# Attention in a fused attention, routing and expert kernel: value products in two column tiles, scores issued three heads early, other PSUM users moved to the outputs' ring, and work moved off VectorE

## The chip, the cores and the metric

The kernel runs on one core of one Trainium2 chip. The metric is the time of one execution in device microseconds. Five engines work side by side: TensorE (PE in the profile, with its weight loads as PEld), VectorE (DVE), ScalarE (ACT), GpSimd (POOL) and SyncE (SP), which here only issues DMAs. Each engine takes its instructions in program order; what one engine needs from another is ordered by semaphores.

## The reference

```
scores = scale * q @ k^T                # 2 batches, 8 heads, 768 positions, 64 per head
keep   = (key < 4) | (0 <= query - key < 128)
a      = exp(scores - max) over keep;  a = a / (sum(a) + 1e-9)
x      = a @ v                          # laid out as 1536 tokens x 512
logits = x @ w_gate                     # 8 experts
route: walk the 12288 logits from the largest; a token takes the first expert
       that still has room (192 tokens per expert)
y      = relu(x[of e] @ w1[e]) @ w2[e]  # 8 experts, 512 -> 1024 -> 512
h      = y @ w_in;  out = (h * sigmoid(h)) @ w_out     # 512 -> 2048 -> 512
```

The inputs are float32 (`w_in` and `w_out` come as 64-bit words and are unpacked to float32 on the chip).

## The kernel before

The program has four parts one after the other: attention (`attention_band`, L196 to L484), routing by repeated counting (`Route`), the experts, and the feed-forward layer (`ffn`). While the attention runs, the first weights are loaded and unpacked.

**Tiles.** Attention works on 12 tiles of 128 queries (`NT`; i = 0 to 11, six per batch). A query block sees its own key block, the block on its left (if it is not the first of its batch, `j` = 0) and four sink keys. The loop at L441 counts heads, n = 8 i + h, one step per head, and runs on for 18 steps after the last of the 96 heads, to let the later stages finish. One step issues, for several heads at different distances behind n:

- `s_mm(n)` (L257), every fourth step: the scores of four heads, as 32 small products (16 when j = 0) in 64x64 tiles of the array, into two banks of the PSUM ring "s", which has four banks. [...]
- `s_exp(n - 2)` (L296) on ScalarE: the exponential.
- `tr(n - 5)` (L310): a transpose on TensorE into the ring "tp"; after each fourth head ScalarE copies the four results out (L321) and GpSimd masks them into a diagonal part `atd` (L323) and a left part `at` (L326).
- `s_merge` (L281) on VectorE joins the two score pieces of a head, and `s_max(n)` (L287) adds the mask and finds the maximum, one per head.
- `sink_tr` (L342): once per tile the sink weights are transposed into a bank of "s" and copied out by VectorE (`ats`, L346).
- `pv(n - 13)` (L350): the value products of one head, `d` with the own block (L361) and `f` with the left block (L363), each 128 rows by 128 columns of weights with 73 moving columns; at each fourth head one sink product for all four (L366), into a bank of the ring "X" (two banks). Then `finish` (L370): VectorE takes the reciprocal of the sums (L388), the weighted logits `lw` (L384), their sum `L` (L391) and the scaled output `x` (L395). For the last two tiles ScalarE does the scaling.
- `vw`, `vw_tr`, `sinks` (L399 to L428), at steps given by the table `VWS`: v times the gate's weights, by which the logits come with the value products. They also take their PSUM from "s" through `misc` (L330).

Small steps of VectorE and ScalarE wait in short lists (`dve_now`, `dve_bg`, `act_now`, `act_bg`, `act_late`) and are issued one or two at a time by `feed` (L430).

**The start.** VectorE clears an array `zero` (L334) that the warm-up products read (`warm`, L338): eight products of 512 columns ahead of the first scores and two at each of the next five steps (`WARM`, L193). Their results are not used.

**Loads.** All loads go through SP's queue in program order. `load` brings keys and queries of a tile, `load_v` (L213) two arrays for the values. Through `hooks` the loop also calls `Weights.load` for seven buffers, at steps 18, 20, ..., 30 (`FIRST`, L887), and `Weights.unpacked` at the 40 steps in `EVEN` and `ODD` (27 to 91), which issues one step of unpacking on VectorE: five steps (`s0` to `s4`, L930 to L949) for each of eight quarters. When a buffer is unpacked the next piece of weights is loaded into it.

**Behind the attention** the routing starts while the last tiles are still at work (`plan`, L1588), and at its end TensorE begins the experts.

Of the kernel before, what the change touches and what calls it, by code (L numbers as in the profile page):

```python
# [11 lines left out]
F32 = mybir.dt.float32  # L12
# [173 lines left out]
LT, LP, LS = 5, 13, 6  # L186
LATE = 9, 10
VWS = {8: [((0, (0,)), 0)], 10: [((0, (0,)), 1)], 11: [((0,), 2)], 13: [((0, (1,)), 0)], 16: [((0, (1,)), 1)],
       58: [((1,), 2)]}
for m in range(1, NT // 2):  # L190
    VWS[2 * H * m + 5], VWS[2 * H * m + 8] = [((m,), 0)], [((m,), 1)]
PB = {"s": 4, "tp": 2, "X": 2}
WARM = (8,) + (2,) * 5  # L193


def attention_band(tc, qd, kd, va_d, vt_d, vs_d, sel_d, wbd_d, eye_d, n_sink, ident, x_d, L_sb, pp, hooks={}):  # L196
    nc = tc.nc
    with ExitStack() as ctx:
# [14 lines left out]
        def load_v(i):  # L213
            b, j = divmod(i, NB)
            if i % 2 == 0:
                vts[i // 2] = wp.tile([P, 4, 2, P], F32, name="vt", bufs=2)
            nc.sync.dma_start(vts[i // 2][:, :, i % 2], vt_d[b, j])
            nc.sync.dma_start(va[:, j], va_d[b, j])
# [12 lines left out]
        load_v(0)  # L231
        nc.sync.dma_start(vsf[0][:96], vs_d[:96, 0])
        load_v(1)
        load(2)
        vsr = [cp.tile([97, H, VW], F32R, name=f"vsr{b}") for b in range(B)]
# [106 lines left out]
        def sink_tr(i):  # L342
            tp = misc()[:96]
            nc.tensor.transpose(tp, A.pop((i, "s")).rearrange("p r h s -> p (r h s)").bitcast(F32), ident)
            if i < NT - 1:
                dve_now.appendleft(lambda: nc.vector.tensor_copy(ats[i % 2][:96], tp))  # L346
            else:
                act_now.appendleft(lambda: nc.scalar.activation(ats[i % 2][:96], tp, AF.Copy))

        def pv(n):  # L350
            i, h = divmod(n, H)
            b, j = divmod(i, NB)
            g, r = divmod(h, 4)
            if r == 0:
                if (i, g) == (NT - 1, 0):
                    X[i, g] = misc(HH * VW).rearrange("p (h v) -> p h v", h=HH)
                else:
                    X[i, g] = pp.tile([P, HH, VW], F32, name="X", bufs=PB["X"])
# [5 lines left out]
            if r < 3:  # L364
                return
            nc.tensor.matmul(X[i, g], ats[i % 2], vsr[b][:, g * HH:(g + 1) * HH], start=False, stop=True,  # L366
# [3 lines left out]
        def finish(i, g):  # L370
# [17 lines left out]
            dve_now.append(lambda: nc.vector.reciprocal(rv, xp[:, :, D + E]))  # L388
# [1312 lines left out]
```

## Time and profile before

| | us |
|---|---|
| median of 3 runs | 551.68 (550.93 to 551.82) |
| the profiled execution, its own time | 551.16 |
| its span, first to last instruction | 549.4 |
| TensorE busy in the span | 529.3 |
| VectorE busy | 352.0 |
| ScalarE busy | 293.2 |
| GpSimd busy | 228.5 |

The profile is of one execution. Times are microseconds from the start of the span. A line such as L361 is a line of the kernel. "x24" counts instructions; a line of the timeline merges neighbours of one kind and gives the start of the first and the time until the last has ended. Instructions on one engine overlap in their ends, so what one costs in a dense stretch is the distance from its start to the next one's start, not how long it lasts. A float32 matrix product appears as two instructions. Idle time stands in brackets with what ended it.

### The profile page before, as it was taken

Reading aid. Unit: us, or ns where it says so; the run is one execution under the profiler, and the core shown is the slowest. Engines: PE = TensorE matmul, PEld = TensorE weight load, DVE = VectorE, ACT = ScalarE, POOL = GpSimd, SP = SyncE. Lnnn points to the kernel's source line nnn. Section 1 sums busy time; section 2 is a strip of 40 time slices with the busy share of each in tenths; the row PEclk is TensorE's granted clock in tenths of the full one; section 3 lists DMA queues with packets and bytes.
Section 4 is the critical chain, followed back from the end, with each engine's and each line's share of the span. In section 5 each row is a group of like instructions: output and inputs, shape, how many; then the busy total and the mean of one; then the engine's idle time right before and its main releaser. Section 6 shows DMA issues by size and latency. Waiting matters only on the chain.

```text
span 549.4 us, 10689 instructions
## 1 busy us (share of the span) xinstructions
PE 529.3 (96%) x3901; PEld 480.2 (87%) x3901; DVE 352.0 (64%) x983; ACT 293.2 (53%) x576; POOL 228.5 (42%) x219
## 2 busy tenths in 40 slices
PE   8999899878999999999999999999999999999995
PEld 4788688757999999999999998988889899888884
DVE  3798999672443443343338898777979776853523
ACT  4555555655776776786654564443544344443330
POOL 4444354377699999999992000000000000000304
PEclk9999999799999999999999999999999999999999
DMA  7999843155466666666760554553676756265502
GB/s 213 359 391 320 278 162 110 39 197 161 153 210 217 226 227 219 227 222 222 226 184 1 209 201 161 215 161 108 219 263 219 277 173 225 91 241 203 202 17 115
DMA packets 43939, 107.98 MB, mean 197 GB/s; under 512 B 4650, under 2 KB 12458, under 8 KB 43884
## 3 DMA queue, kind: packets, MB, share of 16 engines
q1 hardware_dynamic: 41696, 100.88, 54.1%
q0 software_dynamic: 1920, 6.29, 3.3%
q8 instruction: 31, 0.51, 0.4%
q14 instruction: 24, 0.20, 0.1%
q10 hardware_dynamic: 268, 0.10, 0.1%
HBM read 86.81 MB, written 20.45 MB: 195 GB/s over the span
## 4 chain that ended last, share of the span: by engine, by line
PE 69%; issue 4%; POOL 2%; DMA 1%; ACT 0%; DVE 0%; POOLq 0%; another core or an unknown queue 0%; DVEq 0%; ACTq 0%
PE h L1294 21%; PE acc L1416 21%; PE mm L1200 9%; PE m L1223 8%; PE mm L1203 4%; PE m L1226 4%; POOL out L1387 2%; PE mm L1223 1%; PE mm L1159 1%; DMA row<-x_d,idx 1%; PE mm L1226 1%; PE m L1200 0%; POOLq L1697 0%; PE m L1159 0%; ACT wr L976 0%
## 5 line engine op out<-in xcount | busy, mean ns | idle before, releaser
L979 POOL TENSOR_TENSOR wr<-raw,wr 128x1024 fp32r<-128x1024 f32 x64 | 150.8, 2386 | 9.1 <-ACT wr L976 8.9
L1416 PE MATMUL acc<-wr,gt 128*128 128x512 f32 x576 | 145.4, 395 | 0.0
L1416 PEld LDWEIGHTS acc<-wr,gt 128*128 128x128 f32 x576 | 107.3, 188 | 19.5
L1387 POOL DMA_INDIRECT out<-raw,idx x12 | 11.6, 964 | 241.4 <-DVE raw L1428 241.1
L1294 PE MATMUL h<-x,wr 128*128 128x384 f32 x528 | 101.3, 338 | 0.0
L1294 PEld LDWEIGHTS h<-x,wr 128*128 128x128 f32 x528 | 93.8, 188 | 4.0 <-DVE keep L1328 0.2
L1200 PE MATMUL mm<-xg,wr 128*128 128x384 f32 x248 | 72.4, 360 | 0.5 <-DVE xg L1174 0.3
L976 ACT ACTIVATE wr<-raw 128x1024 fp32r<-128x1024 f32 x64 | 66.8, 1052 | 2.4 <-DMA raw<-in_w 1.3
L1223 PE MATMUL m<-ht,wr 128*128 128x384 f32 x224 | 66.0, 361 | 0.0
L1203 PE MATMUL mm<-xg,wr 128*128 128x192 f32 x248 | 62.2, 251 | 0.0
L1226 PE MATMUL m<-ht,wr 128*128 128x192 f32 x224 | 56.2, 251 | 0.0
L1475 DVE TENSOR_TENSOR gt<-keep,gt 128x384 fp32r<-128x384 f32 x64 | 39.1, 612 | 26.7 <-ACT gt L1281 26.6
L301 ACT ACTIVATE A<-t,nm 128x132 f32<-128x132 f32 x96 | 36.4, 401 | 24.7 <-DVE nm L292 24.4
L1181 DVE TENSOR_TENSOR mm<-mm,t 128x384 f32<-128x384 f32 x33 | 18.7, 566 | 45.2 <-ACT t L1180 45.2
L1200 PEld LDWEIGHTS mm<-xg,wr 128*128 128x128 f32 x248 | 46.5, 188 | 1.2 <-DVE xg L1174 0.7
L1203 PEld LDWEIGHTS mm<-xg,wr 128*128 128x128 f32 x248 | 47.3, 191 | 0.0
L1280 ACT ACTIVATE keep<-keep 128x384 f32<-128x384 f32 x30 | 15.8, 526 | 54.0 <-DVE keep L1328 53.9
L1226 PEld LDWEIGHTS m<-ht,wr 128*128 128x128 f32 x224 | 42.8, 191 | 0.0
L1223 PEld LDWEIGHTS m<-ht,wr 128*128 128x128 f32 x224 | 42.0, 188 | 0.0
L323 POOL TENSOR_SCALAR_AFFINE_SELECT atd<-at 128x512 f32<-128x512 f32 x24 | 17.0, 708 | 50.8 <-ACT at L321 45.7
L1294 PE MATMUL h<-xn,wr 128*128 128x384 f32 x180 | 36.8, 339 | 0.0
L1294 PEld LDWEIGHTS h<-xn,wr 128*128 128x128 f32 x180 | 32.6, 188 | 2.6
(198 smaller groups left out, 931.9 us busy)
## 6 DMA issues: line engine op xcount, KB each, us to landing
raw<-in_w SPq DMA_DIRECT2D x64, 512.0 KB, 4.7
sums_d<-os SPq DMA_DIRECT2D x36, 256.0 KB, 2.0
xn<-mix_d SPq DMA_DIRECT2D x12, 768.0 KB, 5.7
raw<-in_wi SPq DMA_DIRECT2D x16, 512.0 KB, 4.8
raw<-in_wo SPq DMA_DIRECT2D x16, 512.0 KB, 4.7
os<-sums_d SPq DMA_DIRECT2D x24, 256.0 KB, 3.1
mix_d<-xn SPq DMA_DIRECT2D x6, 768.0 KB, 4.7
va<-in_va SPq DMA_DIRECT2D x12, 292.0 KB, 6.1
```

The costliest lines, as they stand in the source:

```text
L301: nc.scalar.activation(A[i][:, h], t, AF.Exp, bias=nm, scale=-1.0)
L976: nc.scalar.activation(w[:, 0, sl], src(), AF.Copy)
L979: (nc.vector if k in self.late else nc.gpsimd).tensor_tensor(w[:, 1, sl], src(), w[:, 0, sl].bitcast(F32), OP.subtract)
L1181: nc.vector.tensor_tensor(h, h, t, OP.add)
L1200: nc.tensor.matmul(mm[:, b, :2 * CAP], w[:, 0, fb, d, o:o + P], x[:, d].rearrange("p a t -> p (a t)"), start=d == 0, stop=False, skip_grou ...
L1203: nc.tensor.matmul(mm[:, b, :CAP], w[:, 1, fb, d, o:o + P], x[:, d, 0], start=False, stop=d == 3, skip_group_check=True)
L1223: nc.tensor.matmul(mm[:, d % 2, :2 * CAP], w[:, 0, d // 2, f, o:o + P], ht[:, f].rearrange("p a t -> p (a t)"), start=c == 0 and f == 0, s ...
L1226: nc.tensor.matmul(mm[:, d % 2, :CAP], w[:, 1, d // 2, f, o:o + P], ht[:, f, 0], start=False, stop=last, skip_group_check=True)
L1294: nc.tensor.matmul(h, w(a, d), x(b, d), start=start and d == 0 and k == 0, stop=d == n - 1 and k == 2, skip_group_check=True)
L1387: i = nc.gpsimd.indirect_dma_start(out=out, out_offset=bass.IndirectOffsetOnAxis(ap=idx[:, t // 3, t % 3:t % 3 + 1], axis=0), in_=o, in_of ...
L1416: nc.tensor.matmul(a, gt[:, u, ts], w[:, v, 2 * p + i], start=(p, i, k) == (0, 0, 0), stop=(p, i, k) == (1, 1, 2), skip_group_check=True)
L1475: later.popleft()()
```

## The change

- **Value products** (`pv`): they are issued once per four heads, at the step in which the last of the four is 14 behind (`LP` 13 to 14), all in a row and followed by the sink product (`pv_sink`). Each product is cut in two, one for the first 64 queries and one for the other 64: 64 columns of weights instead of 128, into partitions 0 to 63 and 64 to 127 of the same bank.
- **Scores**: `s_mm(n + 3)` at steps 1, 5, 9, ..., so three heads ahead of the first one's maximum; only the first group and those of heads 88 and 92 are issued at their own step (`LAST`).
- **PSUM**: `misc` (sink transposes, vw and the like) takes its bank from "X" until step 92, then from "s".
- **VectorE**: for tiles 0 to 7 ScalarE copies the outputs out of PSUM (`taken`), VectorE keeps the reciprocal and the sum `L`, and GpSimd makes `lw` and `x` (`over`). ScalarE takes the sink copy of all tiles, and in `Weights.unpack` the first of the five steps (`s0`) as an absolute value for the eight early quarters.
- **Start**: 62 one-element writes to `zero` on VectorE after it is cleared (`QUIET`), and each warm-up product is cut in five (`WE`).
- **Loads**: `load_v` becomes `load_vt` (two at every second tile) and `load_va`; the seven weight buffers are loaded at steps 17, 25, 33, 45, 53, 60 and 67, and the 40 unpacking steps run from step 37 to 93. In `VWS` vw and its transpose move from 5 and 8 to 7 and 9. A branch hint in `Route.run` is placed one iteration earlier.

```diff
-LT, LP, LS = 5, 13, 6
-LATE = 9, 10
+LT, LP, LS = 5, 14, 6
+LATE, LAST = (9, 10), (88, 92)
+QUIET = 62
...
-    VWS[2 * H * m + 5], VWS[2 * H * m + 8] = [((m,), 0)], [((m,), 1)]
+    VWS[2 * H * m + 7], VWS[2 * H * m + 9] = [((m,), 0)], [((m,), 1)]
...
-WARM = (8,) + (2,) * 5
+WARM, WE = (8,) + (2,) * 5, (0, 104, 208, 312, 412, 512)
...
         def misc(k=P):
-            return pp.tile([P, 512], F32, name="s", bufs=PB["s"])[:, :k]
+            ring = "X" if now[0] < NH - HH else "s"
+            return pp.tile([P, 512], F32, name=ring, bufs=PB[ring])[:, :k]
 
         zero = cp.tile([P, 512], BF, name="zero")
         nc.vector.memset(zero, 0.0)
+        for _ in range(QUIET):
+            nc.vector.memset(zero[:1, :1], 0.0)
...
             for _ in range(k):
-                nc.tensor.matmul(idle, zero[:, :P], zero, start=True, stop=True)
+                for sl in map(slice, WE, WE[1:]):
+                    nc.tensor.matmul(idle[:, sl], zero[:, :P], zero[:, sl], start=True, stop=True)
...
-            if i < NT - 1:
-                dve_now.appendleft(lambda: nc.vector.tensor_copy(ats[i % 2][:96], tp))
-            else:
-                act_now.appendleft(lambda: nc.scalar.activation(ats[i % 2][:96], tp, AF.Copy))
+            act_now.appendleft(lambda: nc.scalar.activation(ats[i % 2][:96], tp, AF.Copy))
...
             f, d = AT[i, g]
-            o = X[i, g][:, r]
-            nc.tensor.matmul(o, d[:, r], va[:, j, h], start=r == 0, stop=False, skip_group_check=True)
-            if j:
-                nc.tensor.matmul(o, f[:, r], va[:, j - 1, h], start=False, stop=False, skip_group_check=True)
...
+            for r in range(HH):
+                for t, c in ((d, j), (f, j - 1))[:2 if j else 1]:
+                    for q in (slice(HB), slice(HB, P)):
+                        nc.tensor.matmul(X[i, g][q, r], t[:, r, q], va[:, c, h + r], start=r == 0 and t is d,
+                                         stop=False, skip_group_check=True)
...
+            if i >= NT - 4:
...
+                return
+
+            xc = wp.tile([P, HH, VW], F32, name="xc", bufs=3)
+
+            def taken():
+                nc.scalar.activation(xc, xp, AF.Copy)
+                at_step[now[0] + 1].append(over)
+
+            def over():
+                nc.vector.reciprocal(rv, xc[:, :, D + E])
+                for o, w in ((lw, slice(D, D + E)), (x, slice(D))):
+                    nc.gpsimd.tensor_tensor(o[:, hs], xc[:, :, w],
+                                            rv.unsqueeze(2).to_broadcast([P, HH, w.stop - (w.start or 0)]), OP.mult)
+                if g == 1:
+                    at_step[now[0] + 4].append(logits)
+                    act_bg.extend(send)
+
+            act_now.append(taken)
...
-            if n < NH and n % 4 == 0:
+            of = n - LP - HH + 1
+            if n == 0 or n in LAST:
                 s_mm(n)
+            elif n % HH == 1 and n + 3 < LAST[0]:
+                s_mm(n + 3)
+            if of % HH == 0 and 0 <= of < NH:
+                pv(of)
+                pv_sink(of)
...
-                if i + 2 < NT:
-                    load_v(i + 2)
+                if i % 2 == 0:
+                    load_vt(i + 2)
+                    load_vt(i + 3)
                 if i + 3 < NT:
                     load(i + 3)
+                load_va(i + 2)
...
-            if k + 1 == nit:
+            if k + 2 == nit:
                 self.foresee("settled")
...
-FIRST, EVEN, ODD = 18, (34, 40, 46, 58, 64, 70, 76, 82, 86), (*range(27, 49, 2), *range(53, 93, 2))
+FIRST, EVEN, ODD = (17, 25, 33, 45, 53, 60, 67), (40, 44, 50, 54, 60, 64, 70, 74, 80, 84, 90), range(37, 94, 2)
...
-                nc.vector.tensor_scalar(box[0][:, sl], word(1), 0x7FFFFFFF, None, OP.bitwise_and)
+                if k in self.early:
+                    nc.scalar.activation(box[0][:, sl].bitcast(F32), word(1).bitcast(F32), AF.Abs)
+                else:
+                    nc.vector.tensor_scalar(box[0][:, sl], word(1), 0x7FFFFFFF, None, OP.bitwise_and)
```

The order of instructions shows two places. The first is TensorE at the second group of the second batch's first tile (s are scores, tp transposes, X value and sink products, s<-ident and s<-vt the sink transpose and vw). Before:

```order
L264 MATMUL s<-kall,qr 64x132 x8
L315 MATMUL tp<-ident,A 128x128
L361 MATMUL X<-va,atd 128x73
L363 MATMUL X<-va,at 128x73
L366 MATMUL X<-vsr_156,ats_171 128x292
L315 MATMUL tp<-ident,A 128x128
L344 MATMUL s<-ident,a_1048 96x128
L403 MATMUL s<-vt,wbd 32x256 x4
L361 MATMUL X<-va,atd 128x73
L363 MATMUL X<-va,at 128x73
```

And in the changed kernel, at the same scores:

```order
L370 MATMUL X<-va,at 64x73 x2
L376 MATMUL X<-vsr_156,ats_172 128x292
L322 MATMUL tp<-ident,A 128x128
L355 MATMUL X<-ident,a_1098 96x128
L322 MATMUL tp<-ident,A 128x128 x3
L271 MATMUL s<-kall,qr 64x132 x8
L370 MATMUL X<-va,atd 64x73 x2
L370 MATMUL X<-va,at 64x73 x2
```

The value products of a head stood between the transposes of later heads; now those of four heads stand in a row behind the scores, in pairs of half the columns, then the sink product, then the transposes together. The sink transpose writes to X instead of s.

The second place is VectorE where the first weights are unpacked (t,nm are maxima, nm reads one out, f unpacking steps). Before:

```order
L388 RECIPROCAL rv<-X 128x4
L292 ISA t,nm<-s,mask 128x132
L292 ISA nm 128x1
L384 TENSOR_TENSOR lw<-X,rv 128x32
L284 COPY_PREDICATED s<-later,s 128x128 x2
L346 CAST ats_172<-s 96x128
L292 ISA t,nm<-s,mask 128x132
L292 ISA nm 128x1
L391 TENSOR_REDUCE L<-lw 128x8
L941 TENSOR_SCALAR f_620<-f_620 128x512
L395 TENSOR_TENSOR x<-X,rv 128x256
```

And in the changed kernel:

```order
L291 COPY_PREDICATED s<-later,s 128x128 x2
L399 TENSOR_REDUCE L<-lw 128x8
L299 ISA t,nm<-s,mask 128x132
L299 ISA nm 128x1
L421 RECIPROCAL rv<-xc 128x4
L993 SCALAR_TENSOR_TENSOR f_1003<-raw,f_1003 128x512
L299 ISA t,nm<-s,mask 128x132
L299 ISA nm 128x1
L291 COPY_PREDICATED s<-later,s 128x128 x2
```

lw, ats and x are gone from VectorE, and the reciprocal reads the copy `xc` in SBUF instead of X in PSUM.

## Rows read from the trace of the kernel before

**Rows 1.** Chain of waits that ended last, share of the span by engine

```profile
PE 69%; issue 4%; POOL 2%; DMA 1%; ACT 0%; DVE 0%; POOLq 0%; another core or an unknown queue 0%; DVEq 0%; ACTq 0%
```

**Rows 2.** Stretches: length, busy per engine, granted clock, DMA share, GB/s

```profile
28.00:42.00 14.00, 13.88 (x217) 12.49 (x220) 14.00 (x72) 8.26 (x22) 7.26 (x14) 1.00 1.05 392
98.00:112.00 14.00, 11.08 (x97) 8.69 (x97) 10.38 (x36) 8.19 (x25) 5.13 (x3) 0.76 0.21 74
154.00:168.00 14.00, 14.00 (x101) 14.00 (x100) 6.40 (x12) 10.62 (x18) 12.65 (x8) 1.00 0.64 209
```

**Rows 3.** Timeline of TensorE: first scores, ninth group, last scores, last sink product

```profile
4.78 1.04 PE L264 MATMUL s<-kall,qr 64*64 64x132 f32 x16
...
30.02 1.45 PE L264 MATMUL s<-kall,qr 64*64 64x128 f32 x32
...
87.87 0.91 PE L264 MATMUL s<-kall,qr 64*64 64x128 f32 x32
...
99.75 0.38 PE L366 MATMUL X<-vsr,ats 97*128 97x292 f32 x1
```

**Rows 4.** Timeline of TensorE: a dense group, vw, value products in a row

```profile
33.18 0.27 PE L315 MATMUL tp<-ident,A 128*128 128x128 f32 x1
33.29 0.34 PE L361 MATMUL X<-va,atd 128*128 128x73 f32 x2
33.47 0.39 PE L363 MATMUL X<-va,at 128*128 128x73 f32 x2
33.78 0.91 PE L264 MATMUL s<-kall,qr 64*64 64x128 f32 x32
...
35.70 0.64 PE L403 MATMUL s<-vt,wbd 128*32 128x256 f32 x8
36.26 0.44 PE L361 MATMUL X<-va,atd 128*128 128x73 f32 x2
...
98.44 0.39 PE L361 MATMUL X<-va,atd 128*128 128x73 f32 x2
98.67 0.39 PE L363 MATMUL X<-va,at 128*128 128x73 f32 x2
```

**Rows 5.** Idle time of TensorE before score products, us and times, until

```profile
  DVE ats L346: 6.6, 9
```

**Rows 6.** Timeline of VectorE, 77 to 81 us, without idle time

```profile
77.80 0.42 DVE L941 TENSOR_SCALAR f<-f 128x512 int32<-128x512 int32 x1
78.14 0.17 DVE L388 RECIPROCAL rv<-X 128x4 f32<-128x4 f32 x1
78.23 0.26 DVE L292 CUSTOM_DVE_ANT_0 t<-s,mask 128x132 f32<-128x132 f32 x1
...
78.42 0.18 DVE L384 TENSOR_TENSOR lw<-X,rv 128x32 f32<-128x32 f32 x1
78.53 0.73 DVE L945 SCALAR_TENSOR_TENSOR f<-raw,f 128x512 int32<-128x512 int32 x1
79.18 0.48 DVE L284 COPY_PREDICATED s<-later,s 128x128 f32<-128x128 int32 x2
79.58 0.41 DVE L395 TENSOR_TENSOR x<-X,rv 128x256 f32<-128x256 f32 x1
79.91 0.28 DVE L292 CUSTOM_DVE_ANT_0 t<-s,mask 128x132 f32<-128x132 f32 x1
...
80.12 0.70 DVE L949 SCALAR_TENSOR_TENSOR f<-raw,f 128x512 int32<-128x512 int32 x1
```

**Rows 7.** Timeline of the start: warm-up products, a one-element write on GpSimd

```profile
1.25 3.59 PE L340 MATMUL tp<-zero 128*128 128x512 bf16 x8 [1.25 <-DVE zero L334]
1.32 0.09 POOL L534 MEMSET r_none<- 1x1 int32 x1
```

**Rows 8.** Groups of ScalarE and GpSimd, 0 to 100 us: busy, mean ns, idle before

```profile
L301 ACT ACTIVATE A<-t,nm 128x132 f32<-128x132 f32 x96 | 36.4, 401 | 24.7 <-DVE nm L292 24.4
...
L323 POOL TENSOR_SCALAR_AFFINE_SELECT atd<-at 128x512 f32<-128x512 f32 x24 | 17.0, 708 | 50.8 <-ACT at L321 45.7 <-PE tp L315 3.0 <-PE s L344 2.2
```

More of the change, by code (lines that the diff above doesn't have):

```diff
@@ L1 @@
 import math
-from collections import deque
+from collections import defaultdict, deque
 from functools import partial
@@ L230, in attention_band @@
         load(1, 2)
-        load_v(0)
+        load_vt(0)
+        load_va(0)
         nc.sync.dma_start(vsf[0][:96], vs_d[:96, 0])
-        load_v(1)
+        load_vt(1)
         load(2)
+        load_va(1)
         vsr = [cp.tile([97, H, VW], F32R, name=f"vsr{b}") for b in range(B)]
@@ L352, in pv, with pv_sink @@
             b, j = divmod(i, NB)
[L353 to L358, printed above, removed]
-            f, d = AT[i, g]
-            o = X[i, g][:, r]
-            nc.tensor.matmul(o, d[:, r], va[:, j, h], start=r == 0, stop=False, skip_group_check=True)
-            if j:
-                nc.tensor.matmul(o, f[:, r], va[:, j - 1, h], start=False, stop=False, skip_group_check=True)
-            if r < 3:
-                return
-            nc.tensor.matmul(X[i, g], ats[i % 2], vsr[b][:, g * HH:(g + 1) * HH], start=False, stop=True,
+            g = h // HH
+            if (i, g) == (NT - 1, 0):
+                X[i, g] = misc(HH * VW).rearrange("p (h v) -> p h v", h=HH)
+            else:
+                X[i, g] = pp.tile([P, HH, VW], F32, name="X", bufs=PB["X"])
+            f, d = AT[i, g]
+            for r in range(HH):
[3 more added lines that the diff above has]
+                                         stop=False, skip_group_check=True)
+        def pv_sink(n):
+            i, h = divmod(n, H)
+            g = h // HH
+            nc.tensor.matmul(X[i, g], ats[i % 2], vsr[i // NB][:, g * HH:(g + 1) * HH], start=False, stop=True,
                              skip_group_check=True)
@@ L438, in attention_band @@
         act_now, act_bg, act_late, dve_now, dve_bg = (deque() for _ in range(5))
+        at_step, now = defaultdict(list), [0]
         warm(WARM[0])
         NH = NT * H
-        for n in range(NH + LP + 5):
+        for n in range(NH + LP + 4):
             i, h = divmod(n, H)
-            if n < NH and n % 4 == 0:
+            now[0] = n
+            dve_now.extend(at_step.pop(n, ()))
+            of = n - LP - HH + 1
+            if n == 0 or n in LAST:
                 s_mm(n)
+            elif n % HH == 1 and n + 3 < LAST[0]:
[3 more added lines that the diff above has]
+                pv_sink(of)
             if n < len(WARM) - 1:
@@ L932, in s0 @@
                     box.append(self.fresh())
-                nc.vector.tensor_scalar(box[0][:, sl], word(1), 0x7FFFFFFF, None, OP.bitwise_and)
+                if k in self.early:
+                    nc.scalar.activation(box[0][:, sl].bitcast(F32), word(1).bitcast(F32), AF.Abs)
+                else:
+                    nc.vector.tensor_scalar(box[0][:, sl], word(1), 0x7FFFFFFF, None, OP.bitwise_and)
             def s1(sl=sl):
@@ L1551, in fused @@
                 hooks = {NT * H // 2: [load_route]}
-                for k in range(W.raws):
-                    hooks.setdefault(FIRST + 2 * k, []).append(W.load)
+                for n in FIRST:
+                    hooks.setdefault(n, []).append(W.load)
                 for n in sorted({*EVEN, *ODD}):
```

35 lines of the change are left out of this document (19 added, 16 removed).

## The prediction

> **What bounds the kernel now.** I read the chain of waits first [rows 1]: TensorE holds 69% of it, nearly all in the expert and feed-forward lines, so from the experts to the end the kernel is TensorE's own work. The stretches say the same [rows 2]: from 154 to 168 us TensorE is busy 14.00 of 14. None of those lines is edited; that part can only begin earlier or later. What the change can move is the attention, from the first score to the last value product [rows 3]: 4.78 to about 100 us, 24 groups of four heads. There TensorE is busy 13.88 of 14 us and VectorE 14.00 of 14 [rows 2]. A busy TensorE is not yet a bound, so I priced its work by start-to-start times.
>
> A group with a left neighbour costs TensorE [rows 4]: scores 0.9 (33.78, 32 instructions); four cycles of one transpose and two value products, each 0.11 + 0.18 + 0.22 = 0.51; a sink product 0.22; in all 3.2, and with the odd users of its queue (a sink transpose, vw) 3.45. Where value products follow each other, one costs 0.22 (98.44 to 98.67). VectorE's prices, again start to start, in a stretch without idle time [rows 6]: a step of the weights' unpacking 0.34 (77.80 to 78.14), a reciprocal 0.09, lw 0.11, a longer unpacking step 0.65, two merges 0.40, x 0.33, a maximum 0.21. The sink copy ats and the sum L work on as many columns or fewer than a maximum: 0.2 each, one per two groups. A group is 4 x 0.21 + 0.80 + 0.09 + 0.11 + 0.33 + 0.2 = 2.37, and where unpacking runs (8 quarters of three short and two long steps, 2.3 each, over 16 groups) 3.5. The groups come 3.86 apart there: (87.87 - 30.02) / 15 [rows 3]. So two engines at 3.45 and 3.5 share a ring of score banks and hold each other up: TensorE waited 6.6 us for a bank that a sink copy on VectorE had to free [rows 5].
>
> **The change, part by part.**
>
> *Value products in two column tiles.* 176 pairs (96 diagonal, 80 left) become 352 products of 64 columns of weights. One price is 0.22 now. Nothing in the trace shows this shape. If the two tiles run side by side, each loads half as many columns: 0.11. If they go one after the other, the columns loaded are the same: 0.22, no gain. The nearest row is vw, the same full height in column tiles: 256 moving columns, four tiles, 0.56 us until the next instruction (35.70 to 36.26) [rows 4], which for 73 columns scales to 0.16. I take 0.15. A group then costs 0.9 + 8 x 0.15 + 0.22 + 4 x 0.11 = 2.76, plus switches of tile shape, plus 0.25 of odd users. A switch shows today between the last value product (33.47 + 0.22) and the scores (33.78): 0.09. A group gets one more, so I count 0.15 for all: 3.15.
>
> [...]
>
> *Scores three heads early, odd users out of their ring.* The wait for a bank that the sink copy frees goes [rows 5]. Two groups of scores stay in flight, and TensorE does value products and transposes while VectorE takes maxima. What is late next is the outputs' ring of two: a product group now queues behind the copy of the one before it, on ScalarE; behind that wait stand the transposes and the next scores. It costs at most one exponential, 0.40 [rows 8], when it happens.
>
> *VectorE relieved.* Gone: 16 x at 0.33, 16 lw at 0.11, 11 ats at 0.2, 8 unpacking steps at 0.34: 12 us. A group falls to 1.83, with unpacking (2.0 a quarter, over 14.5 groups) to 2.9. ScalarE takes 16 copies of 292 columns, 11 ats and 8 absolute values of 512; at one to two times an exponential's 0.40 for 132 columns that is 14 to 28 us, and it idled 24.4 us waiting for maxima alone [rows 8]. GpSimd takes 32 small products, at most 0.71 each by its 512-wide select, 23 us; it idled 50.8 us before those selects. Both hide; without that cover a late select holds the value products, nine heads later, so a microsecond is absorbed.
>
> *A later start.* 62 one-element writes on VectorE stand before the array that the warm-up products read, each waiting for the last. TensorE's first product, at 1.25 us, waits for them, and the eight warm-up products take until 4.78 [rows 7]. No such VectorE row exists. GpSimd's one-element write takes 0.09 [rows 7]; the cheapest VectorE step is the reciprocal's 0.09 [rows 6]. I take 0.09: 5.6 us. Bounds: half of it, 2.8, and a maximum's 0.21, 13. The warm-up in 40 pieces streams the same columns: nothing.
>
> *Loads.* Weights' loads spread over heads 17 to 67 instead of 18 to 30; on SP's queue the value loads now stand behind the next keys and queries. The loads were densest from 28 to 42 us, at 392 GB/s [rows 2], where the weights' loads were bunched; spread out they ask for less at a time, and no group is due earlier in the first 30 us than now. Nothing. The branch hint one iteration earlier is one register read on TensorE: nothing.
>
> *The sum*, against the profiled execution's own 551.16 us:
> 1. start: +5.6 (2.8 to 13).
> 2. first score to the ninth group, 25.2 us now: the first two intervals 3.4 with the warm-up between, six at 2.8 = 16.8: 20.2, so -5.0 (0 to -7).
> 3. the 15 intervals to the last scores: at 3.3 (3.15 and some coupling) 49.5 for 57.85: -8.3 (3.05 gives -12.1, 3.65 gives -3.1).
> 4. tail, 87.87 to 100.13: 34 pairs x 0.07 = -2.4, a group's products now come in one block a step later, +1.2: -1.2.
>
> -8.9: 542.3 us. The median of the runs stood 0.5 above the profiled one; I forecast **542.5** us.
>
> [...]
>
> **The rivals.**
> - *A larger gain* (13%): pairs at 0.11 and cheap writes. VectorE then bounds at 2.9, groups 3.05 apart: +2.8 - 6 - 12.1 - 2.2 = -17.5, 533.5 us. The vw row speaks for it; the price of small VectorE steps against.
> - *Coupled engines* (10%): TensorE, VectorE, ScalarE and GpSimd pass each group round; if the ring of two outputs stalls it, groups stay 3.65 apart: +5.6 - 3 - 3.1 - 0.5 = -1.0, 550 us. For it: 3.86 today over two engines that need 3.5. Against: today's waits are the score ring's [rows 5].
> - *Loads in a line, slower* (9%): the pair stays at 0.22, because the four loads of 64 columns follow each other. TensorE then needs 3.45 + 0.15 = 3.6, with the coupling 3.8 a group: +5.6 - 1.5 - 0.9 + 0.3 = +3.5, 554.5 us. It decides from a pair price of about 0.20 up, where the groups' gain no longer pays for the start. For it: at 0.22 today the weights are the price, and their columns do not get fewer. Against: vw, and the scores' 32 loads in 0.9 us. [...]
> - *It does nothing* (2%): start and relief cancel, 551.5 us.
>
> **How the numbers follow.** The forecast (536 to 549 us) has 66%, the rivals the rest. A measurement of this kernel tells 0.2%, 1.1 us, from no change. Faster: 66 + 13 and half of the coupled case, 84%. Same: a third of that case and the last, 5%. Slower: 11%. The range, 533 to 553 us, leaves out the ends of the largest gain and of the slower rival.
>
> **What would show it.** Right: groups of scores about 3.3 us apart after the ninth; a pair of tiles at 0.15 us; the first score near 10.4 us; last value product near 91; VectorE below 90% in the middle; the experts' part unchanged in length. Wrong: a pair at 0.20 or more; one-element writes far from 0.09; TensorE waiting for the copy on ScalarE; or a low granted clock inside the attention, where TensorE would have fallen idle.

## The result and the profile after

The changed kernel took **557.8 us** (median of 4 runs, 557.5 to 558.0) against 551.8 us of the kernel before, measured on the same chip: a ratio of 1.0099, 95% interval 1.0075 to 1.0122. It is 6 us slower. The prediction was 542.5 us, faster, with a range of 533 to 553: wrong in sign and outside its range.

The profiled execution has a span of 556.2 us against 549.4. The page gives busy time per engine, and the granted TensorE clock in 40 slices:

```profile
PE 523.4 (94%) x4325; PEld 472.8 (85%) x4325; DVE 344.0 (62%) x994; ACT 301.8 (54%) x611; POOL 245.0 (44%) x251
...
PEclk9999999899999999999999999999999999999998
```

The same three stretches as in [rows 2], of the changed kernel:

```profile
28.00:42.00 14.00, 13.02 (x288) 10.62 (x286) 7.83 (x54) 9.68 (x30) 9.38 (x23) 1.00 0.76 249
98.00:112.00 14.00, 9.76 (x158) 8.32 (x153) 10.64 (x45) 8.44 (x28) 3.52 (x9) 0.88 0.22 77
154.00:168.00 14.00, 14.00 (x103) 14.00 (x103) 5.67 (x11) 9.67 (x16) 13.14 (x6) 1.00 0.60 200
```

The experts' part is as full as before. In the attention VectorE, which was at 14.00 of 14, now has 7.83, and TensorE 13.02 instead of 13.88. No engine is full any more, yet nothing is faster. The milestones that answer to [rows 3] and [rows 7], first VectorE's start, then TensorE:

```profile
1.26 7.12 DVE L344 MEMSET zero<- 1x1 bf16 x62
```

```profile
8.43 3.60 PE L351 MATMUL tp<-zero 128*128 128x104 bf16 x40 [8.43 <-DVE zero L344]
11.95 1.16 PE L271 MATMUL s<-kall,qr 64*64 64x132 f32 x16
...
32.41 1.23 PE L271 MATMUL s<-kall,qr 64*64 64x128 f32 x32
...
94.07 0.92 PE L271 MATMUL s<-kall,qr 64*64 64x128 f32 x32
...
107.44 0.40 PE L376 MATMUL X<-vsr,ats 97*128 97x292 f32 x1
```

Below, s(n) is the start of the scores of heads n to n+3, "last sink product" the start of the last line above. The first score comes 7.2 us later than before, s(32) 2.4 later (though it is issued three steps sooner), s(92) 6.2 later, the last sink product 7.7 later. From there to the experts the changed kernel is 0.9 us shorter, at least in part by the clock: the kernel before had 6.8 us at half clock in that part, from 101.1 us on (granted clock 0.50), and the changed kernel has none there. In all sixteen profiles below, the routing from the last sink product to the flag that ends it takes 23.5 to 24.1 us where no half clock falls into it (four profiles) and 24.3 to 25.9 in the others. Its own stretch at half clock, 3.4 us from 102.3 us on, falls ahead of the last sink product, in the attention's tail (the clock is the column before the last two):

```profile
102.00:106.00 4.00, 4.00 (x69) 3.67 (x63) 1.72 (x7) 3.51 (x12) 2.03 (x6) 0.57 0.00 1
```

That is the whole +6.8 of the span.

Between s(32) and s(80) the groups come 3.80 us apart ((78.05 - 32.41) / 12), at full clock, before 3.79. What TensorE waits for there is in the chain of one group, around 50 us:

```profile
49.56 0.30 PE L370 MATMUL X<-va,at 128*64 128x73 f32 x4
49.78 0.40 PE L376 MATMUL X<-vsr,ats 97*128 97x292 f32 x1
...
50.31 0.41 ACT L417 ACTIVATE xc<-X 128x292 f32<-128x292 f32 x1 [0.90 <-PE tp L322]
...
50.75 0.18 DVE L421 RECIPROCAL rv<-xc 128x4 f32<-128x4 f32 x1 [1.18 <-ACT xc L417]
50.85 0.27 DVE L299 CUSTOM_DVE_ANT_0 t<-s,mask 128x132 f32<-128x132 f32 x1
...
51.18 0.44 PE L271 MATMUL s<-kall,qr 64*64 64x132 f32 x4 [0.44 <-DVE nm L299]
...
51.46 0.28 DVE L299 CUSTOM_DVE_ANT_0 t<-s,mask 128x132 f32<-128x132 f32 x1
...
51.80 0.67 PE L271 MATMUL s<-kall,qr 64*64 64x132 f32 x12 [0.18 <-DVE nm L299]
```

Read it down. TensorE ends a group of value products with the sink product. ScalarE copies the result to xc (the profile names the transpose that follows, but the copy reads X, whose last product ends at 50.18). VectorE's next instruction is the reciprocal of that copy, and VectorE stands 1.18 us for it, though two maxima of the group in work are behind it in its queue and have their data. Those two maxima free the two score banks that the next scores need, because scores issued three heads early ask for the banks when these maxima are still to come. And behind these scores on TensorE stand the next value products. So each group's value products wait for the value products of the group before, through three engines: a **loop**. Over 32 to 82 us it shows in the waits (total, times, longest):

```profile
DVE rv L421 <- ACT xc L417: 12.3, 10, 2.0
...
PEld s L271 <- DVE nm L299: 7.5, 14, 1.0
```

A second loss is at s(84) to s(88): 8.0 us instead of 4.1 before. Most of it lies in the order of issue: s(84) is issued three heads early, at step 81, s(88) at its own step 88, so seven steps stand between them instead of four, and at 3.80 us per four steps that is 6.65 us. The lead that the early scores had is given back here. The rest goes with a wait of 1.78 us. TensorE, ScalarE and VectorE there:

```profile
87.47 0.38 PE L322 MATMUL tp<-ident,A 128*128 128x128 f32 x2
89.62 0.64 PE L435 MATMUL X<-vt,wbd 128*32 128x256 f32 x8 [1.78 <-ACT ats L356]
90.19 0.91 PE L271 MATMUL s<-kall,qr 64*64 64x128 f32 x32
```

```profile
89.00 0.41 ACT L308 ACTIVATE A<-t,nm 128x132 f32<-128x132 f32 x1 [0.85 <-DVE nm L299]
89.32 0.25 ACT L356 ACTIVATE ats<-X 96x128 fp32r<-96x128 f32 x1
```

```profile
87.63 0.68 DVE L989 SCALAR_TENSOR_TENSOR f<-raw,f 128x512 int32<-128x512 int32 x1
88.24 0.48 DVE L291 COPY_PREDICATED s<-later,s 128x128 f32<-128x128 int32 x2
88.67 0.29 DVE L299 CUSTOM_DVE_ANT_0 t<-s,mask 128x132 f32<-128x132 f32 x1
```

vw, an odd user that the change put into the outputs' ring, waits for a slot of X that the sink copy ats must free; ats stands on ScalarE behind an exponential, which waits for a maximum, which stands on VectorE behind an unpacking step. The scores of group 88, which LAST keeps at their own step, stand behind vw.

### The profile page after: what moved, and what is told of

Its sections match the earlier page's. It is cut to its first block, busy times and chain, and to the rows that moved or that the text cites. A ratio compares the mean times of both kernels' runs of the same rounds, so it can differ in the third digit from the quotient of the medians.

```text
span 556.2 us, 11563 instructions
## 1 busy us (share of the span) xinstructions
PE 523.4 (94%) x4325; PEld 472.8 (85%) x4325; DVE 344.0 (62%) x994; ACT 301.8 (54%) x611; POOL 245.0 (44%) x251
## 4 chain that ended last, share of the span: by engine, by line
PE 68%; issue 4%; POOL 2%; DMA 1%; ACT 0%; DVE 0%; POOLq 0%; DVEq 0%; ACTq 0%
PE h L1338 21%; PE acc L1460 20%; PE mm L1244 9%; PE m L1267 8%; PE mm L1247 4%; PE m L1270 4%; POOL out L1431 2%; PE mm L1267 1%; PE mm L1203 1%; DMA row<-x_d,idx 1%; PE mm L1270 1%; PE m L1244 0%; POOLq L1741 0%; PE m L1203 0%; ACT wr L1020 0%
## 5 line engine op out<-in xcount | busy, mean ns | idle before, releaser
L308 ACT ACTIVATE A<-t,nm 128x132 f32<-128x132 f32 x96 | 35.9, 400 | 15.7 <-DVE nm L299 15.4
L1325 ACT ACTIVATE gt<-keep 128x384 fp32r<-128x384 f32 x64 | 33.7, 527 | 2.0
```

The costliest lines, as they stand in the source:

```text
L308: nc.scalar.activation(A[i][:, h], t, AF.Exp, bias=nm, scale=-1.0)
L1325: nc.scalar.activation(gt[:, 0], h, AF.Copy)
```

## The experiments

In the diffs "-" is the kernel named first, "+" the experiment. All ratios are to the kernel before, measured beside it. "Flag" is the one-element reduction badi on VectorE that ends the routing; "branch" the conditional that follows it on all engines.

| run | first score | s(32) | us a group, s(32) to s(80) | last sink product | flag to first expert product | ratio (95%) |
|---|---|---|---|---|---|---|
| before | 4.78 | 30.02 | 3.79 | 99.75 | 7.39 | 1 |
| after | 11.95 | 32.41 | 3.80 | 107.44 | 7.66 | 1.0099 (1.0075-1.0122) |
| e1 | 11.96 | 31.82 | 3.61 | 105.08 | 12.00 | 1.0142 (1.0117-1.0166) |
| e2 | 4.78 | 28.61 | 3.80 | 103.69 | 11.03 | 1.0153 (1.0119-1.0186) |
| e3 | 11.96 | 32.50 | 3.80 | 109.07 | 7.62 | 1.0149 (1.0126-1.0172) |
| e4 | 11.95 | 36.96 | 3.74 | 106.14 | 11.11 | 1.0197 (1.0167-1.0227) |
| f1 | 10.33 | 29.34 | 3.48 | 100.56 | 7.59 | 0.9988 (0.9964-1.0011) |
| f2 | 4.78 | 29.03 | 3.53 | 99.72 | 7.75 | 0.9963 (0.9934-0.9992) |
| f3 | 4.78 | 27.32 | 3.81 | 102.45 | 7.61 | 1.0061 (1.0041-1.0081) |
| f4 | 11.78 | 32.81 | 4.33 | 116.37 | 7.49 | 1.0291 (1.0253-1.0328) |
| g1 | 4.78 | 27.15 | 3.49 | 96.44 | 7.60 | 0.9957 (0.9934-0.9980) |
| g2 | 4.37 | 32.19 | 3.94 | 103.48 | 10.21 | 1.0098 (1.0066-1.0130) |
| g3 | 9.40 | 31.36 | 4.93 | 123.66 | 11.06 | 1.0409 (1.0355-1.0464) |
| g4 | 11.88 | 33.92 | 3.47 | 99.67 | 7.65 | 0.9997 (0.9972-1.0022) |
| **h1** | 4.64 | 27.97 | 3.41 | 95.47 | 7.79 | **0.9880 (0.9845-0.9916)** |
| h2 | 11.95 | 35.79 | 3.59 | 104.49 | 7.62 | 1.0054 (1.0028-1.0080) |

From the first expert product to the end all sixteen profiles take 416.9 to 417.5 us, so the columns hold all that differs, but for the routing between last sink product and flag (23.5 to 25.9).

### e1: the reciprocal later

The reciprocal and GpSimd's two products go three steps behind xc.

```diff
-                at_step[now[0] + 1].append(over)
+                at_step[now[0] + 3].append(over)
```

> The changed kernel, with the reciprocal of a group (and GpSimd's two products behind it) issued three steps behind the copy xc instead of one, so that it stands behind the maxima of its own group on VectorE. Theory A (a loop: last product of a group on TensorE, copy xc on ScalarE, reciprocal on VectorE ahead of two maxima, those maxima free the score bank, next scores): the VectorE idle time that ends with xc goes from 10.8 us in 32-82 to under 2, score groups s(32) to s(84) come 3.3 to 3.5 us apart instead of 3.83, and the time falls by 4 to 6 us to 552 to 554. Theory B (the pace is set by VectorE's or TensorE's own work, or by loads): groups stay 3.8 apart, 557.8 within 1 us.

The mechanism came as theory A has it. The same waits over 32 to 82 us:

```profile
PEld s L271 <- DVE nm L299: 2.8, 6, 1.2
...
DVE rv L421 <- ACT xc L417: 0.9, 1, 0.9
```

From s(32) to s(64) the groups come 3.35 us apart ((58.65 - 31.82) / 8), 3.86 in the changed kernel. But the run is not faster. Two things took it back. TensorE fell idle around 62 us, and its clock was granted at half from 65 to 72 us:

```profile
60.00:64.00 4.00, 2.62 (x56) 2.07 (x56) 3.97 (x16) 2.36 (x7) 1.42 (x4) 1.00 1.04 395
64.00:68.00 4.00, 4.00 (x75) 3.50 (x67) 4.00 (x25) 2.64 (x8) 3.18 (x8) 0.64 1.04 410
68.00:72.00 4.00, 4.00 (x37) 2.54 (x31) 3.46 (x17) 1.52 (x6) 3.38 (x6) 0.51 1.07 370
```

And between the flag and the experts it lost 4.3 us: TensorE's first product behind the branch, in the changed kernel and in e1:

```profile
133.44 2.32 PE L1199 MATMUL mm<-wr 128*128 128x512 f32 x9 [0.53 <-DVEq L784]
```

```profile
134.97 4.18 PE L1199 MATMUL mm<-wr 128*128 128x512 f32 x9 [3.62 <-DVEq L784]
```

The branch on VectorE's queue, again of the changed kernel and of e1 (the event that follows it is what TensorE waits for):

```profile
L784 DVEq EVENT_SEMAPHORE  x2: 21/21/21, 133.3 to 133.4; - x2
...
L784 DVEq COMPARE_BRANCH  x1: 72/72/72, 132.7 to 132.7; - x1
```

```profile
L784 DVEq EVENT_SEMAPHORE  x2: 21/21/21, 134.8 to 134.9; - x2
...
L784 DVEq COMPARE_BRANCH  x1: 72/72/72, 131.1 to 131.1; - x1
```

VectorE gets through the branch in 0.6 us in the one and in 3.7 in the other, with nothing to wait for in the records.

### e2: without the one-element writes

```diff
-QUIET = 62
+QUIET = 0
```

> The changed kernel without the 62 one-element writes ahead of the warm-up. The late start costs 7.2 us at the first score (11.95 against 4.78). Theory A (attention is a chain from its first score on): nearly all comes back, last sink product near 101, 551 us. Theory B (the first groups wait for keys and values that land when they land, so that the late start is half hidden, as s(32) is only 2.4 us later than before): s(32) near 30, 554 to 556. Either way the stretch at the low clock in the routing part may move.

Theory B in the attention: of 7.2 us, 3.8 come back at s(32) and 3.75 at the last sink product. They are lost again at the branch (TensorE waits 3.51 us there, and then runs at half clock for 3.4 us), so the time does not fall at all, which neither theory had.

### e3: the last odd users back in the scores' ring

```diff
-            ring = "X" if now[0] < NH - HH else "s"
+            ring = "X" if now[0] < 84 else "s"
```

> The changed kernel, with the last odd users (sink transpose of block 9, last values' weights and their transposes) back in the scores' ring from step 84 instead of the outputs' ring. Theory A (TensorE stands 1.8 us at 87.8 because a slot of X waits for the copy ats): s(84) to s(88) takes 5.5 to 6 us instead of 8.0 and the time falls by 2 to 2.5, to 555.5. Theory B (VectorE is late there, with outputs and unpacking between its maxima, and the slot only shows it): s(88) stays within 0.7 us of 90.2 and the time within 1 us of 557.8.

s(84) to s(88) takes 7.5 us (82.27 to 89.73), which is where theory B put s(88); its time, unchanged, did not come, the run is slower than the changed kernel (1.0149 against 1.0099). The slot of X was only the link through which the wait reached TensorE. s(88) to s(92) became 6.7 instead of 3.9, part of it at half clock (92 to 99 us).

### e4: the kernel before with a late start

```diff
         nc.vector.memset(zero, 0.0)
+        for _ in range(62):
+            nc.vector.memset(zero[:1, :1], 0.0)
```

> The kernel before with the same 62 one-element writes ahead of its warm-up, nothing else. First score near 12. Theory A (the start is on the chain in full): last sink product near 107, 558 to 559 us. Theory B (early groups wait for their loads anyway): s(32) is 2 to 4 us later, not 7, and the time 553 to 556.

Here, as theory A has it, the late start is paid nearly in full: s(32) 6.9 us later, the last sink product 6.4. Of the 9.1 us by which the span is longer, another 3.7 are the branch again: 11.11 us from the flag to the first expert product, TensorE waiting 3.18 at it.

### f1, f2, f3: where the writes stand, and VectorE's branch

Counted in the traces, 586 recorded instructions of VectorE stand ahead of the branch in the changed kernel, 605 in the kernel before, 585 in e3: 0.6 us each. In e2 it is 524, in e1 608, in e4 667: over 3 us each. This count is called the branch's place below. f1 is e1 with 48 writes instead of 62, which puts the branch at place 594. f2 is e1 with the 48 writes on a tile of their own:

```diff
+        pad = cp.tile([1, 1], BF, name="pad")
         for _ in range(QUIET):
-            nc.vector.memset(zero[:1, :1], 0.0)
+            nc.vector.memset(pad, 0.0)
...
             of = n - LP - HH + 1
+            if n in range(4, 32):
+                nc.vector.memset(pad, 0.0)
```

with QUIET = 20. f3 is the changed kernel with its 62 writes in this form (20, then 42 steps), the reciprocal untouched.

> The changed kernel with the reciprocal three steps behind xc and 48 one-element writes instead of 62. Theory P (VectorE's branch behind the routing waits 3.6 us when its place in VectorE's program is bad: place 586, 605 and 585 went through in 0.6 us, 524, 608 and 667 waited 3.2 to 3.6): its place is now 594, the branch takes 0.6 us, and from the flag badi to the first expert product it is 7.5 us instead of 12.0. With the start 1.6 us earlier the time is 553 to 555. Theory Q (the wait at the branch comes from when it is reached, or from transfers beside it): the wait stays near 3.6 us and the time near 558.

> As the run before, with the 48 one-element writes on a tile that TensorE does not read (20 at the start, then one a step for 28 steps), so that the warm-up need not wait for them. Theory A+P: first score near 4.8, score groups 3.3 to 3.5 us apart from s(32), last sink product near 98 to 100, branch 0.6 us, 546 to 549 us: faster than both kernels. Rival (the early groups wait for keys, so that the start gives back 2 to 3 us at most): last sink product 101 to 103, 550 to 552.

> The changed kernel with its 62 one-element writes on a tile that TensorE does not read (20 at the start, one a step for 42 steps), the reciprocal where the change has it. The place of VectorE's branch stays 586. Theory A+P: first score near 4.8, last sink product near 103.7 as in the run without the writes, but the branch takes 0.6 us: 552.5 to 554. Theory Q: as without the writes, 557 to 560.

Theory P held three times of three: 7.6 to 7.75 us from the flag to the first expert product. VectorE's branch in f1:

```profile
L784 DVEq EVENT_SEMAPHORE  x2: 21/21/21, 128.2 to 128.3; - x2
...
L784 DVEq COMPARE_BRANCH  x1: 72/72/72, 127.6 to 127.6; - x1
```

The time came 2 to 4 us better than expected for f1, and for f2 in the rival's range, though its last sink product is where theory A had it. f2 starts 5.5 us before f1 and has 0.3 of that left at s(32): with the start early, VectorE stands for the mask that GpSimd makes, and TensorE for queries (1.6 us at once, between 5 and 28 us), and TensorE runs at half clock from 15 to 22 us, where f1 does not.

```profile
5.64 0.30 DVE L299 CUSTOM_DVE_ANT_0 t<-s,mask 128x132 f32<-128x132 f32 x1 [2.22 <-POOL mask L256]
```

f3 against the changed kernel is the price of where the writes stand: 5.0 us at the last sink product in the profiled executions, about 2 us by the ratios of 1.0061 and 1.0099. f3's time, 555.4 us, is 1.4 above the range expected. For the branch the kernel needs a count of writes that puts it at a good place (48 do with the reciprocal late, f1), not writes that the warm-up waits for.

### f4: the column tiles undone

```diff
-                    for q in (slice(HB), slice(HB, P)):
+                    for q in (slice(P),):
```

> The changed kernel with the values' products undivided (128 columns again), all else as changed. VectorE's program is the same. Theory A (the values' products lie on the loop, which has no slack): a group is longer by eight pairs at 0.22 instead of 0.126, so 0.75 us, groups s(32) to s(84) come 4.5 us apart instead of 3.83, last sink product 12 to 17 us later, 570 us. Rival (the pace is set by VectorE's or ScalarE's own work or by loads, TensorE has slack): under 4 us later, 558 to 562.

Theory A in kind, 2.5 us under its time: groups 0.53 us further apart (0.67 expected), last sink product 8.9 us later (12 to 17 expected). A full product and a pair of tiles, in f4 and in the changed kernel, start to start between rows:

```profile
60.39 0.39 PE L370 MATMUL X<-va,atd 128*128 128x73 f32 x2
60.61 0.39 PE L370 MATMUL X<-va,at 128*128 128x73 f32 x2
```

```profile
49.05 0.30 PE L370 MATMUL X<-va,at 128*64 128x73 f32 x4
49.18 0.30 PE L370 MATMUL X<-va,atd 128*64 128x73 f32 x4
49.30 0.29 PE L370 MATMUL X<-va,at 128*64 128x73 f32 x4
```

0.22 against 0.125: the tiles do what they say.

### g1: scores of group 88 early too

f2, with

```diff
-LATE, LAST = (9, 10), (88, 92)
+LATE, LAST = (9, 10), (92,)
```

> As the run with late reciprocal and writes on their own tile (550.77 us), and the scores of group 88 issued three heads early too (only group 92 at its own step), so that they stand ahead of the product vw, whose slot of X TensorE waits for at 81-82. Theory A (that wait stops the scores): s(84) to s(88) takes 4 to 5 us instead of 7.7, the last sink product comes 2 to 3 us earlier, near 97, and the time is 547 to 549. Theory B (VectorE has too much to do there: outputs, unpacking): the wait moves to group 92, last sink product within 1 us of 99.7, 550 to 551.

s(84) to s(88) falls from 7.75 to 4.5 us, but s(88) to s(92) is now 7.6 (76.75 to 84.39): the seven steps moved one group on, and the wait with them, as theory B has it. The last sink product comes 3.3 us earlier than in f2, as theory A has it, but 2.1 of these stood already at s(84) (72.21 against 74.29), ahead of all that the edit touches; 1.2 are left for the edit. The profiled execution spans 545.8 us, the median is 549.9, between the two theories.

### g2: the column tiles alone

The kernel before, its products in column tiles, head by head where they were:

```diff
-            o = X[i, g][:, r]
-            nc.tensor.matmul(o, d[:, r], va[:, j, h], start=r == 0, stop=False, skip_group_check=True)
-            if j:
-                nc.tensor.matmul(o, f[:, r], va[:, j - 1, h], start=False, stop=False, skip_group_check=True)
+            for t, c in ((d, j), (f, j - 1))[:2 if j else 1]:
+                for q in (slice(HB), slice(HB, P)):
+                    nc.tensor.matmul(X[i, g][q, r], t[:, r, q], va[:, c, h], start=r == 0 and t is d,
+                                     stop=False, skip_group_check=True)
```

> The kernel before with the values' products in two column tiles of 64, head by head at their old place, nothing else. If VectorE sets the pace before (97% busy, the copy ats waits behind its maxima): s(32) to s(92) keeps its 57.9 us within 1.5, time 550.5 to 552.5. If TensorE's products set it (pair 0.126 instead of 0.22, eight pairs a group): 0.75 us less a group, 10 us over the sixteen groups, 541 to 544.

A miss for both: it is slower, groups 3.94 us apart. One head and the next transpose on TensorE:

```profile
49.44 0.27 PE L315 MATMUL tp<-ident,A 128*128 128x128 f32 x1
49.64 0.35 PE L362 MATMUL X<-va,atd 128*64 128x73 f32 x4
49.82 0.30 PE L362 MATMUL X<-va,at 128*64 128x73 f32 x4
50.04 0.33 PE L315 MATMUL tp<-ident,A 128*128 128x128 f32 x1
```

Going into the tiles the transpose takes 0.20 (0.26 at the next one) instead of 0.11 until the next start and the first pair 0.18, and the last pair takes 0.22 instead of 0.125 on the way out. A head costs 0.60 to 0.66 us, 0.51 before [rows 4]: two switches a head eat more than the tiles give, and TensorE is busy 14.00 of 14 us from 28 to 42. This run also lost 2.8 us behind the flag, at another engine's branch: VectorE's, at place 605, went through, and TensorE's own took 1.86 us instead of 0.48, after which the clock was at half from 130 to 137 us.

### g3: the outputs on VectorE

```diff
-QUIET = 62
+QUIET = 40
...
-            if i >= NT - 4:
+            if i >= 0:
```

> The changed kernel with the outputs of all blocks on VectorE, read from X as before (no copy xc on ScalarE, no products on GpSimd), and 40 one-element writes so that VectorE's branch stays at a good place. VectorE has 0.6 us more of work a group (lw 0.18, x 0.42), but the loop is shorter by the copy xc (0.41 and its hand-over). Theory A (loop): groups stay 3.7 to 3.9 us apart, start 2.5 us earlier, 554 to 558. Theory B (VectorE's relief is what carries the changed kernel): groups 4.3 to 4.5 us apart, 562 to 566.

Worse than both: groups 4.93 us apart, part of it at half clock (50 to 54 and 74 to 88 us). The loop is not shorter for want of the copy: the reciprocal now waits for the sink product itself, 16.3 us over 32 to 82, and all the work of the outputs follows ahead of the maxima. As far as this run shows, with 17 us at half clock in it, this order of scores needs the outputs off VectorE.

```profile
DVE rv L402 <- PE X L376: 16.3, 10, 2.4
```

Its branch fell at place 610, not at a good one as meant, and TensorE waited 3.55 us there: 3.4 of its loss.

### g4: scores at their own step

```diff
-            if n == 0 or n in LAST:
-                s_mm(n)
-            elif n % HH == 1 and n + 3 < LAST[0]:
-                s_mm(n + 3)
+            if n < NH and n % HH == 0:
+                s_mm(n)
```

> The changed kernel with each group's scores at their own step again, not three heads early; all else as changed, VectorE's program the same. Theory A (TensorE waits for the score banks because the early scores ask for them while two maxima of the group before are still behind the reciprocal): TensorE's wait for nm, 14 us in 36-96, is under 4 us, groups 3.3 to 3.6 us apart, 550 to 554. Theory B (early scores are needed, without them VectorE waits for scores at every group): groups 4.0 to 4.4 us apart, 560 to 566.

Theory A: over 36 to 96 us the wait of the scores' weight loads for nm is 1.3 us instead of 8.9, groups are 3.47 apart, s(80) to s(92) takes 12.0 us instead of 16.0, and the last sink product comes 7.8 us earlier than in the changed kernel, at 99.67, though the start is still late. (1.3 us of this are the tail, which has no half clock here.) VectorE still stands for xc, but for 4.1 us, and TensorE no longer behind it; over 32 to 82 us, as above:

```profile
DVE rv L421 <- ACT xc L417: 4.1, 6, 1.2
...
PEld s L271 <- DVE nm L299: 1.3, 5, 0.4
```

### h1 and h2: the loop cut

h1 is f2 with the scores of g4; h2 is g4 with the undivided products of f4.

> The run with late reciprocal and writes on their own tile (550.77 us), with every group's scores at their own step as well. Theory A (early scores and the early reciprocal are two ends of one loop, so cutting it twice adds little): groups near 3.4 us apart as with either cut, the stall at group 88 is gone with the early order (g4: 78.5 to 83.6 to 87.6), last sink product 94 to 96, time 545 to 548. Theory B (two costs that add): groups 3.1 us apart, last sink product 90 to 92, 541 to 543. Theory C (own-step scores make VectorE wait once TensorE is not late from the start): last sink product 98 to 100, 550.

> The changed kernel with scores at their own step and the values' products undivided (128 columns): neither of the two edits to TensorE's order and tiles that the loop goes through. Theory A (with the loop cut TensorE's own work sets the pace: 3.0 us a group tiled, 3.75 undivided): groups 3.8 us apart instead of 3.4, last sink product 106 to 110, 558 to 562. Theory B (with the loop cut TensorE has slack and VectorE or GpSimd sets the pace): within 2 us of 551.5, so that the column tiles were worth something only inside the loop.

h1 is theory A: 3.41 us a group, last sink product 95.47, 546.4 us. Late reciprocal and own-step scores cut one loop, and what h1 has over g4 is the start (s(32) at 27.97 instead of 33.92), of which 4.2 us are left at the last sink product. It beats both kernels, by 1.2% and, by the two ratios, 2.2%. h2 lies between its theories: 0.12 us a group, 4.8 us at the last sink product, a ratio of 1.0054 against 0.9997. With the loop cut the tiles are worth about half of what they are worth inside it by the last sink product (4.8 against 8.9 us), and a quarter by the pace (0.12 against 0.53).

## Why the prediction was wrong

The sum said -8.9 us against the profiled execution; the spans say +6.8. Its steps:

1. **Start: +5.6 predicted, +7.2 measured.** A one-element write takes 0.115 us (7.12 / 62), not 0.09; the mechanism was right. That it is paid in full was not said to depend on anything, and it does: nearly all of it in the kernel before (e4), 5.0 us (f3) or 3.75 (e2) in the changed one.
2. **First score to the ninth group: 20.2 predicted, 20.46 measured.** Right in size. The sum does not say that s(32) is now issued at step 29, three steps sooner than before, a lead that is given back in step 3; as far as this lead made the size right, it was luck.
3. **The 15 intervals to the last scores: 49.5 predicted, 61.66 measured, 12.2 of the 15.7 us by which the sum is off.** This is the step that failed, in two halves. In the 12 intervals to s(80) the pace is 3.80 instead of 3.3: 6.0 us. The last three take 16.0 instead of 9.9: 6.1 us. These hold 15 steps, not 12, because s(80) is issued at step 77 and s(92) at step 92: three steps at 3.80 per four are 2.85 us that the sum had at nothing; the slower pace of the other twelve is 1.5, and 1.8 are the wait at s(88). The terms under it were right or too cautious: a pair at 0.125 where 0.15 was taken, VectorE far below full. What was missed is the order. "What is late next is the outputs' ring of two" named the wrong ring for the pace (over 32 to 82 us no value product waits for xc, and vw does for 1.2 us in all): it is the score ring, which the text counted as relieved. It took the wait for a bank behind the sink copy [rows 5] as the only one there, and did not ask what else would stand on VectorE ahead of the maxima that free a bank. A reciprocal had stood among the maxima before too, but it read X without a copy between, and scores at their own step asked for banks of the group before the last; now it waits for ScalarE, and the early scores ask for the bank at that moment. Cutting this at either end (e1 as far as s(64), f1, g4) gives 3.35 to 3.48 us a group, near the pace that was predicted. The rival of coupled engines, given 10%, had the kind right, with another ring and 550 us.
4. **Tail: -1.2 predicted, +1.5 measured** (s(92) to the end of the last sink product, 13.77 against 12.26). Most of the +1.5 is the clock, one of the signs that the prediction named for being wrong: TensorE stands in the tail, as here behind an exponential, and then its clock is at half from 102.3 to 105.8 us, where a pair takes 0.24 us (104.40 to 104.88 for two) instead of 0.125.

```profile
100.44 0.33 PE L322 MATMUL tp<-ident,A 128*128 128x128 f32 x1 [1.36 <-ACT A L308]
```

The runs show what it costs. From s(92) to the start of the last sink product the runs with tiles in one block take 12.0 to 12.1 us where the clock stays full (f2, g1, g4) and 13.3 to 13.4 where it is at half for 3.4 us (after, e2, f1, f3, g3, h1): 1.3 us. (e3, with 2.7 us at half clock, takes 12.6, e1, with 5.8, 14.4.) With undivided products and full clock it is 13.4 (f4, h2). So the tiles do save in the tail, 1.4 us where the sum had 2.4, and the rest of the change costs 1.6 (13.4 against 11.88 before) where the sum had 1.2. g4, at full clock:

```profile
87.61 0.91 PE L271 MATMUL s<-kall,qr 64*64 64x128 f32 x32
...
99.67 0.40 PE L376 MATMUL X<-vsr,ats 97*128 97x292 f32 x1
```

The slower rival, loads in a line, did not come: the tiles come at 0.125 a pair, with as many columns loaded as an undivided product at 0.22 (f4).

The switch of tile shape was priced at 0.06 to 0.09 and is 0.09 to 0.15 a time in g2 (a transpose 0.20 to 0.26 instead of 0.11 on the way in, a last pair 0.22 instead of 0.125 on the way out). The change pays two a group because it also gathers four heads' products into one block, g2 pays two a head: the gathering, which the prediction mentioned only as a delay in the tail, is what makes the tiles pay.

Loads, ScalarE and GpSimd were costed at nothing, and that stands as far as amount goes; ScalarE's place in the loop is what it did not cost. The branch was not in the sum and had no part in the difference of these two profiles (7.39 and 7.66 us), but added 2.8 to 4.3 us to five of the fourteen experiments. The branch hint was costed at nothing too; TensorE's own branch took 0.39 to 0.41 us in the thirteen kernels with the earlier hint, and 0.48, 0.82 and 1.86 us in the three without it (before, e4, g2). No run changed the hint alone, so that the hint does this is not shown.

Not settled: why the clock falls in some executions and not in others after the same idle time, and how much of the stall at s(88) is VectorE's unpacking; no run took that away alone.

## What to carry to other kernels

When work moves off a full engine, write down for each buffer in a ring which instruction frees it and what stands ahead of that instruction in its queue, after the change: a small instruction that waits for another engine, put ahead of a large one that frees a buffer, ties the engines into a loop that no busy share shows (here 3.80 us a group with the loop, 3.35 to 3.48 with it cut). Issuing work earlier asks for its buffer earlier; that is a gain only if the buffer is free by then. And when an edit moves anything ahead of a branch, compare the time across the branch before blaming the edit: two runs here (e1, e2) had an attention shorter by 2.4 and 3.75 us and no better time, because of 4.3 and 3.4 us more behind the flag. Read the granted clock of two stretches before comparing their times, too: 3.4 us at half clock in one tail hid the 1.4 us that the tiles save there.

## What the runs showed of the hardware

**The branch depends on where it stands in VectorE's program.** Over all sixteen profiles: branches with 585, 586 (five times), 594 (four times) and 605 (twice) recorded instructions of VectorE ahead of them went through in 0.6 us; those with 524, 608, 610 and 667 made TensorE wait 3.2 to 3.6. One-element writes far ahead of it, which do nothing else, moved it from one to the other. The good places, 585 to 605, lie together here, with bad ones on both sides; no run shows why.

**A write of one element takes 0.115 us** when the next writes the same element, on VectorE: 62 took 7.12 us in the changed kernel and in e4; 20 of them on their own tile took 2.28 (f2).

**The granted clock falls at other times in every run.** It fell to half at 65 us in e1, where TensorE had been idle for 1.1 of the 3 us before, and stayed at full in the changed kernel at 90 us, after 1.8 idle of 3. e1 has stretches at half from 65, 85, 99 and 133 us, f4 none before the last 3 us. In the attention such a stretch costs: s(72) to s(76) in e1, at half clock, took 5.6 us, and 3.5 in f1, where only the first 0.3 us of it were. In the tail 3.4 us at half clock cost 1.3.
